# Natural query order, one store per unit, and a reordered seven-product step in a fused attention and MLP kernel

## The chip, the cores and the metric

The kernel runs on one core of one Trainium2 chip. The time is device microseconds of one execution. A profile's *span* is the core's own busy interval in one profiled execution and is one or two microseconds shorter than the run's time (315.5 against 317.19 us for the changed kernel). All readings below compare fast runs with fast runs. A *ratio* is the mean time of one kernel's fast runs over that of the other's fast runs of the same rounds, so it is not quite the ratio of the medians that stand beside it.

## The reference

Sliding-window attention over 8 batches of 576 positions, 8 heads of 64, then a two-layer MLP on the 4608 resulting rows.

```python
def _attn_ref(q, k, v):                       # (8, 8, 576, 64) each
    scores = (1/sqrt(D)) * q @ k^T
    scores = where(|pos_q - pos_k| <= 32, scores, -1e9)
    attn = softmax(scores)
    return attn @ v

def _moe_ref(x, w_in, w_out):                 # x (4608, 512), w_in (512, 2048), w_out (2048, 512)
    h = x @ w_in
    g = h * sigmoid(1.702 * h)
    return g @ w_out
```

## The kernel before

The rows are cut into 36 *units* of 128 and 18 *pairs* of units (a tile of 256 rows). A step of the main loop (`window(w)`, here "pair w") computes attention of pair w, the second layer of pair w−2, and the first layer of pair w−1. Queries are transposed in four groups (`JT = 4`, row = 4s + j), so the scores of a block of 64 queries come out ordered by (j, s) and not by row.

Before, that permuted order was kept through to the output, and the store undid it in two DMAs of 64 rows:

```python
    def scores(self, u):                     # (matmuls cut)
        for eo in range(2):
            if u < self.NU - 1:
                nc.scalar.activation(p[:, eo], sc[eo], AF.Exp, scale=self.scale)
            else: ...                        # last unit: reordered while writing

    def store(self, u, cols=slice(None)):
        nc, row = self.nc, 128 * u + 32
        o_sb = self.o_sb[u]
        if u < self.NU - 1:
            for blk in range(2):
                nc.sync.dma_start(self.out[row + 64*blk:row + 64*blk + 64, cols]
                                      .rearrange("(s j) f -> j s f", j=JT),
                                  o_sb[64*blk:64*blk + 64, cols])
```

The second layer uses seven products instead of eight (a Strassen-like scheme), on sums of `w_out` made once and sums of `g` made per pair on VectorE. Products 1, 6, 7 and 4 accumulate in one PSUM bank and are copied out ("kept") in between, so product 6 must wait until product 1 has been copied, 7 until 6 has, and 4 until 7 has. Products 5 and 3 accumulate in a second bank. Product 2 has a third. The banks have kinds: "a" has four, "h" two, "o" and "t" one each. The first layer takes the two "h" banks in turn.

```python
        self.scores(a); self.scores(b)
        self.product(t, 1, "o"); self.keep(t, 1, dve)
        self.product(t, 5, "h")              # stays in one of the two "h" banks ...
        self.gelu_table()
        self.product(t, 6)
        self.band(a, 0); self.keep(t, 6, dve); self.band(a, 1)
        run(kt)                              # key transposes, bank "t", copied by VectorE
        self.product(t, 2, "h")
        self.band(b, 0); self.result(t, 11); self.band(b, 1)
        self.product(t, 7); self.keep(t, 7, dve)
        self.values(a); self.values(b)
        self.result(t, 22)
        self.product(t, 4); self.result(t, 21, act)
        self.norm(a); self.x_T(a); self.norm(b); self.x_T(b)    # xT: DMA transposes
        self.product(t, 3); self.result(t, 12)                  # ... until here
        run(kt)
        run(l1, 4); self.feed(w); run(l1, 4)                    # first layer, banks "h"
        self.g_sums(w - 1, 1)
```

The softmax here doesn't subtract the row's maximum and nothing guards it: scores larger than these inputs give would overflow.

## Time and profile before

| | before |
|---|---|
| median time | 337.4 us (336.82 to 338.03) |
| TensorE busy | 303.0 us of a 336.6 us span |
| VectorE, ScalarE busy | 212.6, 186.5 us |

These lines of the page of the kernel before carry the rest (group lines: line, engine, operation, tiles, shapes, count, then busy time, mean ns of one, idle time before them and its main releaser; queue lines: packets, MB, time of the packets as a share of 16 engines' span):

```profile
span 336.6 us, 9950 instructions
...
q1 hardware_dynamic: 31296, 16.19, 36.8%
...
L312 PE MATMUL h_ps<-xT,w_in_sb 128*128 128x256 bf16 x1152 | 134.7, 274 | 10.0 <-DMA xT<-x 8.7
...
out_dram<-o_sb SPq DMA_DIRECT2D x68, 128.0 KB
```

TensorE waits 8.7 us ahead of the first layer for transposed activations. The queue that carries stores and transposes (q1) moves 16.19 MB and takes 36.8% of the engines' time for it. The stores are 68 of 128 KB. The pauses of TensorE themselves are shown in the prediction.

### The profile page before, as it was taken

To read this page: it belongs to the slowest core of one execution; us is meant where nothing else is said; L and a number is where in the kernel's file an instruction comes from. 1 tells how busy PE (TensorE), PEld (TensorE's weight loads), DVE (VectorE), ACT (ScalarE), POOL (GpSimd) and SP (SyncE) were. 2 spreads that over 40 slices of the span, in tenths; PEclk is the share of its full clock that TensorE was granted. 3 is DMA by queue.
4 is the path that set the end of the run, shared out by engine and by line. 5 is a ranking of instruction groups with operands and counts; after the bars stand their busy time and mean duration, and the time that the engine had idled before them with its cause. 6 is when DMAs were issued, how large, how long until landed. Compare 5 with 4: busy or idle time off the path is not lost. (4 is left out here: it accounts for less than half of the span.)

```text
span 336.6 us, 9950 instructions
## 1 busy us (share of the span) xinstructions
PE 303.0 (90%) x4224; PEld 247.6 (74%) x4224; DVE 212.6 (63%) x637; ACT 186.5 (55%) x300; POOL 71.2 (21%) x105
## 2 busy tenths in 40 slices
PE   8989999769779969994998899999999999999993
PEld 4668655657668758873887688878888888878882
DVE  2561157788586828683586848686777758583451
ACT  3566354565655638470657365747484847585330
POOL 8972566206014200501040202020200000000000
PEclk9999999999999999998999999999999999999998
DMA  8999999959919996799949994777493442405013
GB/s 141 147 191 203 186 196 189 201 76 122 125 39 134 110 106 91 70 135 102 137 32 146 104 141 47 99 99 97 36 99 84 68 50 48 67 30 72 24 38 89
DMA packets 92684, 35.11 MB, mean 104 GB/s; under 512 B 65248, under 2 KB 88288, under 8 KB 92640
## 3 DMA queue, kind: packets, MB, share of 16 engines
q0 software_dynamic: 61248, 18.22, 57.4%
q1 hardware_dynamic: 31296, 16.19, 36.8%
q8 instruction: 33, 0.54, 0.7%
q14 instruction: 11, 0.09, 0.1%
q10 hardware_dynamic: 96, 0.07, 0.1%
HBM read 36.96 MB, written 9.44 MB: 138 GB/s over the span
## 5 line engine op out<-in xcount | busy, mean ns | idle before, releaser
L312 PE MATMUL h_ps<-xT,w_in_sb 128*128 128x256 bf16 x1152 | 134.7, 274 | 10.0 <-DMA xT<-x 8.7
L312 PEld LDWEIGHTS <-w_in_sb 128*128 128x128 bf16 x1152 | 111.9, 98 | 26.2 <-issue 6.3
L314 ACT ACTIVATE g<-h_ps 128x512 f16<-128x512 f32 x144 | 85.8, 597 | 76.2 <-PE h_ps L312 74.8
L140 POOL DMA_DIRECT2D ve<-in_v_dram x40 | 33.7, 849 | 157.7 <-DVE p L256 114.0
L373 PEld LDWEIGHTS <-gs 128*128 128x128 f16 x512 | 49.7, 98 | 14.3 <-issue 8.6
L373 PE MATMUL o_ps<-w_sum,gs 128*128 128x256 f16 x384 | 49.1, 272 | 6.2 <-DVE part L106 4.8
L353 DVE TENSOR_TENSOR gs<-g 128x512 f16<-128x512 f16 x32 | 13.5, 423 | 63.7 <-ACT g L314 63.6
L241 ACT ACTIVATE p<-sc 128x512 bf16<-128x512 f32 x70 | 36.6, 601 | 6.7 <-PE sc L235 6.4
L106 DVE COPY kT<-tp 128x512 bf16<-128x512 bf16 (+2 forms) x45 | 25.9, 593 | 22.2 <-PE tp L160 20.0
L373 PEld LDWEIGHTS <-g 128*128 128x128 f16 x384 | 34.8, 98 | 4.9 <-ACT g L314 0.2
L373 PE MATMUL o_ps<-w_out_sb,g 128*128 128x256 f16 x256 | 33.3, 273 | 0.0
L284 DVE TENSOR_TENSOR x<-pv,rec 128x256 bf16<-128x256 f32 x72 | 30.6, 425 | 2.5
L106 DVE COPY part<-o_ps 128x256 f32<-128x256 f32 x48 | 20.2, 420 | 15.0 <-PE o_ps L373 14.4
L256 DVE TENSOR_TENSOR p<-p,mask 128x512 bf16<-128x512 bf16 x70 | 28.3, 419 | 1.9 <-ACT p L241 1.6
L106 ACT COPY o_sb<-o_ps 128x256 f32<-128x256 f32 x16 | 6.0, 372 | 37.6 <-PE o_ps L373 30.7
L391 DVE TENSOR_TENSOR o_sb<-o_ps,part 128x256 f32<-128x256 f32 x48 | 20.1, 420 | 0.9 <-PE o_ps L373 0.2
L241 ACT ACT_TABLE_LOAD x15 | 19.2, 1283 | 0.3
L272 PEld LDWEIGHTS <-p 128*64 128x64 bf16 x576 | 12.0, 110 | 9.7 <-DVE p L256 4.2
L272 PE MATMUL pv<-ve,p 128*64 128x65 bf16 x288 | 15.9, 197 | 2.8 <-DVE p L256 1.4
L106 ACT COPY qT<-tp 128x512 bf16<-128x512 bf16 (+1 forms) x17 | 9.6, 573 | 15.4 <-PE tp L160 12.9
L412 ACT ACT_TABLE_LOAD x14 | 18.0, 1283 | 0.3
L235 PEld LDWEIGHTS <-kT 64*64 64x64 bf16 x1152 | 12.1, 108 | 7.6 <-issue 7.2
(68 smaller groups left out, 293.4 us busy)
## 6 DMA issues: line engine op xcount, KB each, us to landing
out_dram<-o_sb SPq DMA_DIRECT2D x68, 128.0 KB
ve<-in_v_dram POOLq DMA_DIRECT2D x32, 128.0 KB, 9.6
w_in_sb<-in_moe_w_in_dram POOLq DMA_DIRECT2D x4, 512.0 KB, 9.7
w_out_sb<-in_moe_w_out_dram POOLq DMA_DIRECT2D x4, 512.0 KB, 12.2
ks<-in_k_dram POOLq DMA_DIRECT2D x2, 448.0 KB, 14.5
qs<-in_q_dram POOLq DMA_DIRECT2D x2, 448.0 KB, 19.4
ks<-in_k_dram POOLq DMA_DIRECT2D x3, 256.0 KB, 17.5
qs<-in_q_dram POOLq DMA_DIRECT2D x3, 256.0 KB, 12.1
```

Source lines behind the costliest of these rows:

```text
L106: (eng.copy if eng is self.nc.scalar else eng.tensor_copy)(out, in_)
L140: self.nc.gpsimd.dma_start(self.ve[m % NV][off:off + n, :, :self.D], self.v[b, :, s:s + n, :].rearrange("h s d -> s h d"))
L241: nc.scalar.activation(p[:, eo], sc[eo], AF.Exp, scale=self.scale)
L256: self.nc.vector.tensor_mul(pv, pv, msk.to_broadcast([128, 4, 2, SQ]))
L272: nc.tensor.matmul(acc[half][blk * 64:blk * 64 + 64, hh, :], p[:, h % 2, h // 2 * 2 + blk, :], vt[:, h, :D + 1], start=(hh == 0), stop=(hh ...
L284: nc.vector.tensor_mul(x[:, hs, :], acc[half][:, :, :D], rec[:, hs, :].to_broadcast([128, 4, D]))
L312: nc.tensor.matmul(hps[:, i, :], self.w_in_sb[:, kr, ff * 128:(ff + 1) * 128], self.xT[t][:, kr, :], start=(i == 0 and kr == 0), stop=(i = ...
L314: nc.scalar.activation(self.g[t][:, ffs[0]:ffs[1] + 1:ffs[1] - ffs[0], :], hps, AF.Gelu_apprx_sigmoid)
L353: dve.tensor_add(s[0], g[:, top, v], g[:, low, v])
L373: nc.tensor.matmul(self.part[t, key], x, y, start=(first and k == 0), stop=(k == 7), skip_group_check=True)
L391: self.nc.vector.tensor_add(dst, self.part[t, src], self.part[t, other])
L412: self.nc.scalar.activation(self.spark, self.spark, AF.Gelu_apprx_sigmoid)
```

## The change

The intent: let ScalarE put the queries back in natural order while it computes the exponential (it reads PSUM at a stride), so that a unit's output is 128 plain rows and one store; put the products in an order that leaves more time to copy each kept product; do both key transposes of a step in one bank and copy them on ScalarE, which is less loaded; make the sums of `w_out` earlier.

```diff
 def scores(self, u):
-            if u < self.NU - 1:
-                nc.scalar.activation(p[:, eo], sc[eo], AF.Exp, scale=self.scale)
-            else: ...
+            nc.scalar.activation(p[:, eo].rearrange("k h (s j) -> k h s j", j=JT),
+                                 sc[eo].rearrange("k h (j s) -> k h s j", j=JT), AF.Exp, scale=self.scale)
 def store(self, u, cols):
-            for blk in range(2):
-                nc.sync.dma_start(self.out[row + 64*blk:row + 64*blk + 64, cols].rearrange("(s j) f -> j s f", j=JT),
-                                  o_sb[64*blk:64*blk + 64, cols])
+            nc.sync.dma_start(self.out[row:row + 128, cols], o_sb[:, cols])
 def head(self):                  # masks in natural order, loads of w_out reordered: cut
+        for n in range(4):       # early, where VectorE idles
+            self.w_sums(n, 0)
 ...
+        for n in range(4):       # after the norm of unit 6
+            self.w_sums(n, 1)
 ...                              # among the key transposes of block 2
-            for half in range(2):
-                self.w_sums(hp, half)
 def window(self, w):             # pairs 5 to 15; pair 4 is changed alike
+        self.g_sums(t, 1, (0, 1))
         self.product(t, 1, "o"); self.keep(t, 1, dve)
-        self.product(t, 5, "h")
+        self.product(t, 2, "h")
+        self.g_sums(t, 1, (2, 3))
+        self.result(t, 11)
         self.gelu_table()
+        self.product(t, 5, "t")
+        self.band(a)
         self.product(t, 6)
-        self.band(a, 0); self.keep(t, 6, dve); self.band(a, 1)
-        run(kt)
-        self.product(t, 2, "h")
-        self.band(b, 0); self.result(t, 11); self.band(b, 1)
+        self.band(b, 0); self.keep(t, 6, dve); self.band(b, 1)
+        self.values(a)
+        if heads:
+            self.keys_pair(heads, act)       # both key transposes, one bank of kind "h"
         self.product(t, 7); self.keep(t, 7, dve)
-        self.values(a)
         self.values(b)
         self.result(t, 22)
         self.product(t, 4); self.result(t, 21, act)
         self.norm(a); self.x_T(a)
+        self.product(t, 3); self.result(t, 12)
         self.norm(b); self.x_T(b)
-        self.product(t, 3); self.result(t, 12)
-        run(kt)
-        run(l1, 4); self.feed(w); run(l1, 4)
-        self.g_sums(w - 1, 1)
+        run(l1, 4); self.g_sums(w - 1, 0); self.feed(w); run(l1, 4)
```

More of the change, by code (lines that the diff above doesn't have):

```diff
@@ L93, in setup_mask @@
         for blks, rows, sign in ((slice(0, 2), lo, 1), (slice(0, 2), hi, -1), (slice(2, 4), lo, -1), (slice(2, 4), hi, 1)):
-            ap = m[rows, blks, :].rearrange("p b (j s) -> p b j s", j=JT)
+            ap = m[rows, blks, :]
             pool.affine_select(out=ap, in_=ap, compare_op=ALU.is_ge, fill=0.0, base=0,
-                               pattern=[[0, 2], [-sign, JT], [-sign * JT, SQ // JT]], channel_multiplier=sign)
+                               pattern=[[0, 2], [-sign, SQ]], channel_multiplier=sign)
     def cut_mask(self):
-        cut = self.mask.rearrange("p b (j s) -> p b j s", j=JT)
         lo, hi = slice(0, 64), slice(64, 128)
-        for b, rows, cols in ((0, hi, slice(0, 8)), (0, lo, slice(8, 16)), (2, lo, slice(0, 8)), (2, hi, slice(8, 16))):
-            self.nc.gpsimd.memset(cut[rows, b, :, cols], 0.0)
+        for b, rows, cols in ((0, hi, slice(0, 32)), (0, lo, slice(32, 64)), (2, lo, slice(0, 32)), (2, hi, slice(32, 64))):
+            self.nc.gpsimd.memset(self.mask[rows, b, cols], 0.0)
     def cast(self, eng, out, in_):
@@ L239, in scores @@
         for eo in range(2):
-            if u < self.NU - 1:
-                nc.scalar.activation(p[:, eo], sc[eo], AF.Exp, scale=self.scale)
-            else:
-                nc.scalar.activation(p[:, eo].rearrange("k h (s j) -> k h j s", j=JT),
-                                     sc[eo].rearrange("k h (j s) -> k h j s", j=JT), AF.Exp, scale=self.scale)
+            nc.scalar.activation(p[:, eo].rearrange("k h (s j) -> k h s j", j=JT),
+                                 sc[eo].rearrange("k h (j s) -> k h s j", j=JT), AF.Exp, scale=self.scale)
         self.p[u] = p
@@ L252, in band @@
         for eo in range(2) if only is None else (only,):
-            if u < self.NU - 1:
-                pv = p[:, eo].rearrange("p (h b) s -> p h b s", b=2)
-                msk = self.mask[:, a:b + 1:b - a, :].rearrange("p (o b) s -> p o b s", o=1)
-                self.nc.vector.tensor_mul(pv, pv, msk.to_broadcast([128, 4, 2, SQ]))
-            else:
-                for blk, m in ((0, a), (1, b)):
-                    pv = p[:, eo, blk::2, :].rearrange("p h (s j) -> p h s j", j=JT)
-                    msk = self.mask[:, m:m + 1, :].rearrange("p o (j s) -> p o s j", j=JT)
-                    self.nc.vector.tensor_mul(pv, pv, msk.to_broadcast([128, 4, SQ // JT, JT]))
+            pv = p[:, eo].rearrange("p (h b) s -> p h b s", b=2)
+            msk = self.mask[:, a:b + 1:b - a, :].rearrange("p (o b) s -> p o b s", o=1)
+            self.nc.vector.tensor_mul(pv, pv, msk.to_broadcast([128, 4, 2, SQ]))
     def values(self, u, kinds="aa"):
@@ L314, in layer1 @@
         nc.scalar.activation(self.g[t][:, ffs[0]:ffs[1] + 1:ffs[1] - ffs[0], :], hps, AF.Gelu_apprx_sigmoid)
-        if t > 1 and d == 3:
+        if t == 2 and d == 3:
             self.g_sums(t, 0)
@@ L323, in layer2 @@
         o_ps = self.o_ps[u]
-        for ff in range(4 * quarter, 4 * quarter + 4):
+        at = (0, 8, 4, 12)[quarter]
+        for ff in range(at, at + 4):
             nc.tensor.matmul(o_ps, self.g[t][:, ff, s * 128:(s + 1) * 128], self.w_out_sb[:, ff, :],
@@ L329, in layer2 @@
             self.cast(eng or nc.vector, o_sb, o_ps)
-            row = 128 * u + 32
-            for blk in range(2):
-                nc.sync.dma_start(self.out[row + 64 * blk:row + 64 * blk + 64, :].rearrange("(s j) f -> j s f", j=JT),
-                                  o_sb[64 * blk:64 * blk + 64])
+            nc.sync.dma_start(self.out[128 * u + 32:128 * u + 160, :], o_sb)
     def w_sums(self, i, half):
@@ L343, in w_sums, with g_sums @@
         dve.tensor_sub(t[i], a, c)
-    def g_sums(self, t, half):
+    def g_sums(self, t, half, which=range(4)):
         dve, g = self.nc.vector, self.g[t]
-        if half == 0:
+        if t not in self.gs:
             self.gs[t] = self.work.tile([128, 4, self.NFF // 2, 128], F16, name="gs", tag="gs")
@@ L352, in g_sums @@
         u, v = slice(0, 128), slice(128, 256)
-        dve.tensor_add(s[0], g[:, top, v], g[:, low, v])
-        dve.tensor_sub(s[1], s[0], g[:, top, u])
-        dve.tensor_sub(s[2], g[:, top, u], g[:, top, v])
-        dve.tensor_sub(s[3], g[:, low, u], s[1])
+        for n in which:
+            if n == 0:
+                dve.tensor_add(s[0], g[:, top, v], g[:, low, v])
+            elif n == 1:
+                dve.tensor_sub(s[1], s[0], g[:, top, u])
+            elif n == 2:
+                dve.tensor_sub(s[2], g[:, top, u], g[:, top, v])
+            else:
+                dve.tensor_sub(s[3], g[:, low, u], s[1])
     def product(self, t, n, kind=None):
@@ L401, in store @@
         if u < self.NU - 1:
-            for blk in range(2):
-                nc.sync.dma_start(self.out[row + 64 * blk:row + 64 * blk + 64, cols].rearrange("(s j) f -> j s f", j=JT),
-                                  o_sb[64 * blk:64 * blk + 64, cols])
+            nc.sync.dma_start(self.out[row:row + 128, cols], o_sb[:, cols])
         else:
@@ L445, in head @@
         self.cut_mask()
-        for c in range(2):
+        for c in (0, 2):
             self.load_w_out(c)
@@ L449, in head @@
             self.load_heads(1, c)
-        self.load_w_out(2)
+        self.load_w_out(1)
         self.load_v(4, 1)
@@ L551, in head @@
             self.queries_T(2, hp, "o", act)
-            for half in range(2):
-                self.w_sums(hp, half)
             self.layer1(2, 4 + hp)
-        self.g_sums(2, 1)
-        for m in (7, 8, 9):
-            self.odd_v(m, dve)
+        self.odd_v(7, dve)
+        self.g_sums(2, 1, (0, 1))
         for m in (11, 12, 13):
@@ L595, in window @@
             self.keep(t, 1, dve)
-            self.product(t, 5, "h")
+            self.product(t, 2, "h")
+            self.g_sums(2, 1, (2, 3))
+            self.result(t, 11)
+            self.product(t, 5, "t")
+            self.band(7)
             self.product(t, 6)
+            self.odd_v(8, dve)
             self.keep(t, 6, dve)
-            self.band(7)
             self.scores(b)
-            self.product(t, 2, "h")
+            self.values(7)
+            self.odd_v(9, dve)
+            self.norm(7)
             self.band(a)
-            self.result(t, 11)
-            self.values(7)
-            self.norm(7)
+            self.product(t, 7)
             self.gelu_table()
+            self.keep(t, 7, dve)
+            self.result(t, 22)
+            self.values(a)
             self.band(b)
-            self.product(t, 7)
-            self.keep(t, 7, dve)
-            self.values(a)
-            self.values(b)
-            self.result(t, 22)
             self.product(t, 4)
             self.result(t, 21, act)
+            self.values(b)
+            self.product(t, 3)
+            self.result(t, 12)
             self.x_T(7, "t", nc.scalar)
@@ L619, in window @@
             self.x_T(b)
-            self.product(t, 3)
-            self.result(t, 12)
             loads()
@@ L631, in window @@
                 run(l1)
-            self.g_sums(w - 1, 1)
+            self.g_sums(w - 1, 0)
             self.feed(w)
@@ L641, in window @@
             self.scores(b)
+        self.g_sums(t, 1, (0, 1))
         self.product(t, 1, "o")
         self.keep(t, 1, dve)
-        self.product(t, 5, "h")
+        self.product(t, 2, "h")
         if w == 5:
             self.scores(b)
+        self.g_sums(t, 1, (2, 3))
+        self.result(t, 11)
         self.gelu_table()
+        self.product(t, 5, "t")
+        self.band(a)
         self.product(t, 6)
-        self.band(a, 0)
+        self.band(b, 0)
         self.keep(t, 6, dve)
-        self.band(a, 1)
-        run(kt)
-        self.product(t, 2, "h")
-        self.band(b, 0)
-        self.result(t, 11)
         self.band(b, 1)
+        self.values(a)
+        if heads:
+            self.keys_pair(heads, act)
         self.product(t, 7)
         self.keep(t, 7, dve)
-        self.values(a)
         self.values(b)
@@ L665, in window, with keys_pair @@
         self.x_T(a)
+        self.product(t, 3)
+        self.result(t, 12)
         self.norm(b)
         self.x_T(b)
-        self.product(t, 3)
-        self.result(t, 12)
-        run(kt)
         run(l1, 4)
+        self.g_sums(w - 1, 0)
         self.feed(w)
         run(l1, 4)
-        self.g_sums(w - 1, 1)
+    def keys_pair(self, heads, eng):
+        i, at = heads[0][0], (512 * heads[0][0]) % RING
+        tp = self.bank("h", [128, 2, JT, 128], BF16, "tp")
+        for n, (_, hp) in enumerate(heads):
+            for j in range(JT):
+                self.nc.tensor.transpose(tp[:, n, j, :], self.stage["k", i, "c"][:, hp, j], self.ident)
+        for n, (_, hp) in enumerate(heads):
+            for dst, m in ((at, 512),) + (((RING, 64),) if at == 0 else ()):
+                self.cast(eng, self.kT[:, hp, dst:dst + m].rearrange("r (p j) -> r p j", j=JT),
+                          tp[:, n, :, :m // JT].rearrange("r j p -> r p j"))
     def close(self, w, l1):
@@ L679, in close @@
         last = not l1
+        self.g_sums(t, 1)
         for n, kind in ((1, "o"), (2, "a"), (6, None), (5, "a"), (7, None)):
@@ L690, in close @@
             l1.pop(0)()
+        if l1:
+            self.g_sums(w - 1, 0)
         if not last:
@@ L694, in close @@
             l1.pop(0)()
-            self.g_sums(w - 1, 1)
             self.product(t, 3)
```

## The prediction

How much faster one store of 128 plain rows drains than two of 64 permuted rows had been seen in no run. That a strided read of PSUM costs ScalarE nothing rested on the 379 ns of its copy of 256 elements at a stride of 8 bytes; in the same trace a dense copy of 256 elements took it 372 ns. The group lines in the middle have the columns named above. L241 is the dense exponential (601 ns), L243 the one that writes at a stride of 8 bytes (1375 ns), and kT<-tp a copy by VectorE that reads at a stride of 256 bytes (685 ns, where its copies of 512 without a stride took 422 ns in bf16 and 682 ns in f32).

> **What bounds the kernel now.** I read the page's engine line, then the kernel in stretches of one pair of query units (I number them as the main loop does, 4 to 19), then TensorE's timeline where it stands still, then the queue of transfers behind those places. Pairs 6 to 11 (columns after the stretch: its length, then busy time of PE, PEld, DVE, ACT, POOL, granted clock, DMA share, GB/s):
>
> ```profile
> PE 303.0 (90%) x4224; PEld 247.6 (74%) x4224; DVE 212.6 (63%) x637; ACT 186.5 (55%) x300; POOL 71.2 (21%) x105
> ```
> ```profile
> 109.20:128.30 19.10, 15.52 (x225) 13.29 (x224) 12.05 (x39) 9.98 (x16) 1.76 (x2) 1.00 1.66 115
> 128.30:144.30 16.00, 15.59 (x230) 13.42 (x229) 11.56 (x36) 9.98 (x16) 4.94 (x7) 1.00 0.60 77
> 144.30:166.30 22.00, 17.06 (x229) 14.13 (x232) 12.11 (x40) 9.98 (x16) 1.77 (x2) 0.92 1.68 124
> 166.30:182.10 15.80, 15.51 (x229) 13.30 (x230) 11.73 (x38) 9.98 (x16) 3.50 (x4) 1.00 0.76 86
> 182.10:200.50 18.40, 15.69 (x225) 13.20 (x224) 12.35 (x41) 10.07 (x16) 1.76 (x2) 1.00 1.61 118
> 200.50:216.40 15.90, 15.53 (x225) 13.37 (x224) 11.73 (x37) 9.98 (x16) 2.25 (x3) 1.00 0.65 78
> ```
>
> TensorE is the bound: 15.5 us of matmuls in every pair, and a normal pair lasts 16. DVE and ACT have room, so only TensorE's pauses count. Every second pair is longer with the same work, at twice the DMA share. Its pauses:
>
> ```profile
> 121.25 4.00 PE L312 MATMUL h_ps<-xT,w_in_sb 128*128 128x256 bf16 x35 [2.97 <-DMA xT<-x]
> ```
> ```profile
> 157.72 8.61 PE L312 MATMUL h_ps<-xT,w_in_sb 128*128 128x256 bf16 x64 [4.35 <-DMA xT<-x]
> ```
> ```profile
> 193.44 0.83 PE L312 MATMUL h_ps<-xT,w_in_sb 128*128 128x256 bf16 x6 [1.41 <-DMA xT<-x]
> ```
>
> All three wait for the transposed activations xT, a DMA transpose. After the longest, 64 first-layer matmuls spread over 8.34 us instead of 6.99, with 3.4 us of half clock in the clock record. Together 2.97 + 4.35 + 1.35 + 1.41 = 10.1 us. Two more pauses come early, where DVE is behind:
>
> ```profile
> 73.53 1.03 PE L373 MATMUL o_ps<-w_sum,gs 128*128 128x256 f16 x8 [2.55 <-DVE part L106]
> ```
> ```profile
> 87.62 0.40 PE L157 MATMUL tp<-ident,kc 128*128 128x128 bf16 x4 [1.69 <-DVE kT L106]
> ```
>
> Later pairs lose 0.1 to 1.2 us each, before product 5 or 6. Why xT is late, from SP's queue ahead of the 4.35 us pause:
>
> ```profile
> 136.58 1.12 SPq L403 DMA_DIRECT2D out_dram<-o_sb  x2
> 137.81 5.86 SPq L295 DMA_TRANSPOSE xT<-x  x2
> 143.77 1.12 SPq L403 DMA_DIRECT2D out_dram<-o_sb  x2
> 145.61 11.22 SPq L198 DMA_TRANSPOSE qT<-qc  x1
> ```
>
> The trace's packets say more. The first two stores' 128 packets of 2 KB run from 138.4 to 146.0 us, the next two's from 151.2 to 156.2, with only 2.6 to 2.7 in flight. The transpose packets do not start before 143.9, and almost stop between 153 and 156, while the stores drain. Of the second xT's 16 completion counts, ten come at 152.1 us and six only at 156.6 to 157.7.
>
> [...] Each store's DRAM side starts with the dimension of 4[...] (after issue one early update of a store's semaphore, then exactly four).
> [...]
> [...]
> [...]
>
> ```profile
> L241 ACT ACTIVATE p<-sc 128x512 bf16<-128x512 f32 x70 | 36.6, 601 | 6.7 <-PE sc L235 6.4
> ...
> L106 DVE COPY kT<-tp 128x512 bf16<-128x512 bf16 x36 | 24.6, 685 | 22.2 <-PE tp L160 20.0 <-PE tp L157 2.2
> ...
> L243 ACT ACTIVATE p<-sc 128x512 bf16<-128x512 f32 x2 | 2.5, 1375 | 0.0
> ...
> L106 ACT COPY qT<-tp 128x256 bf16<-128x256 bf16 x1 | 0.4, 379 | 0.0
> ```
>
> **The change part by part.**
> Stores. Rows come out in natural order, so two stores of 64 permuted rows become one of 128 plain rows[...]. The bytes stay. The 7.6 and 5 us of draining should fall to 1 or 2, transposes start some 3 us sooner, and the stop at 153 goes. Ten counts of xT were there at 152.1, before the need at 153.15; without the stop the other six should be too. I take 85% of 10.1 us (the loads of q and k, which fill these pairs, stay): -8.6.
>
> Exponentials. They now read PSUM at a stride of 64 bytes and write densely. The copy line of 379 ns read at 8 bytes stride at full rate[...], so I take 601 ns: 0. Unit 35's two slow exponentials go (2 x 0.77) and its four half masks become two whole ones, 4 x 0.586 - 2 x 0.419 = 1.5 us of DVE: inside pair 17 below.
>
> Sums of w_out. Eight DVE operations of 0.683 us stood between the key copies at 63 to 69.7 us, so DVE entered pair 4 late; the sums of g, three shifted copies of v and the first kept product came behind (2.55 us). Now four run around 31 to 36 us, where DVE idles 13.5 us (the needed second w_out load lands at 33.5), and four near 57 to 60, where it idles 1.84. Pair 4's sequence by hand with the trace's durations: product 6 no longer waits, but product 7 waits about 0.35 and the values of unit 8 about 1.6 for norm and mask behind two more copies. From scores to first layer 10.5 us instead of 12.5: -2.0. The 1.69 us pause came of the g sums placed inside that first layer; they move behind it: -1.7. Two pauses of 0.19 among the key transposes of block 2 go: -0.4. Sum -4.1.
>
> Pair 5. Its second scores wait for a small wrap copy at the end of DVE's list, before and after (1.68 us before). By hand I get 1.0 there, 0.9 before the values and 0.4 later: +0.5.
>
> Product order in pairs 6 to 14. Product 2 now precedes 5 and 6, so the kept copy of product 1 is no longer waited for. But one unit's values (0.25 us), not two, lie between product 7 and product 4. A kept copy turns around in 0.31 (product end) + 0.42 + about 0.1 = 0.83 us; 0.25 + 0.11 + 0.03 covers 0.39: a new pause of 0.4 a pair. Before, these nine pairs lost 4.6 us (0.55, 0.41, 0.60, 0.29, 1.25, 0.37, 0.60, 0.16, 0.38); after 9 x 0.45 = 4.05: -0.5.
>
> Key transposes. Both blocks go to one bank, together under product 7's wait, and are copied by ACT: 20 copies of 685 ns leave DVE, 20 of about 585 reach ACT, 1.2 us a pair on an engine with 6 us free: 0. In pairs 15 to 17 there are no key transposes to cover product 7's wait either: 0.85 a pair after, against 0.1, 0.1 and 1.0 before: +1.35.
>
> End. In the last pair the second half of the g sums now follows a result instead of preceding it, so the kept product comes about 0.4 us later: +0.4.
>
> Sum: -8.6 - 4.1 + 0.5 - 0.5 + 1.35 + 0.4 = -10.95. From 337.4: 326.4, say 326.3 us.
>
> **Rivals.**
> Strided reads are slow: if ACT needs 1.3 us an exponential, four last 5.2 us instead of 2.1 in each pair, values wait in 14 pairs, 1.5 us or more each, and the time is near 347. For: [...]the 1375 ns. Against: that one is the write side[...].
> The loads hold xT anyway: pairs 6, 8 and 10 hold both loads of q and k, at a DMA share over 1.6. If they, not the stores, bind, xT gains only 2 or 3 us and the time is 332 to 333. Against: ten of sixteen counts came in time, and odd pairs with the same transposes never wait.
> The early part gains nothing: DVE's work in pair 4 is larger by two copies of v; then some 330.
>
> **Range and chances.** Main term uncertain by 3 us, early part by 2, product order by 2, strided reads a separate tail. Range 320.5 to 332.5. Over 2% faster means under 330.65: 0.82; within 2%: 0.12; slower: 0.06.
>
> **What would show it.** Right: store packets 8 or more in flight; no pause "DMA xT<-x" over 0.5 us in pairs 6, 8 and 10, and no half clock there; exponentials at about 600 ns; DVE busy near 196 us, ACT near 197; pair 4 shorter by some 3.7 us; a pause near 0.4 us before product 4. Wrong: exponentials over 800 ns; pauses for xT that remain while stores are spread; a new wait for the values in every pair.

## The result, and the profile after

The changed kernel took 316.12 us (median of four, 315.69 to 317.19) against 337.37 us of the kernel before in the same rounds; the ratio is 0.9374, interval 0.9346 to 0.9403. The direction was right, but the time lies below the predicted range: 21 us were gained where 11 were predicted.

The page of the changed kernel, the lines that answer to those of before:

```profile
span 315.5 us, 9889 instructions
...
PE 297.6 (94%) x4224; PEld 245.8 (78%) x4224; DVE 201.5 (64%) x611; ACT 195.5 (62%) x324; POOL 71.3 (23%) x105
...
q1 hardware_dynamic: 31584, 16.19, 24.7%
...
L302 PE MATMUL h_ps<-xT,w_in_sb 128*128 128x256 bf16 x1152 | 131.9, 273 | 2.3 <-ACT p L239 0.7
...
L239 ACT ACTIVATE p<-sc 128x512 bf16<-128x512 f32 x72 | 37.5, 602 | 3.8 <-PE sc L234 3.6
...
out_dram<-o_sb SPq DMA_DIRECT2D x34, 256.0 KB, 3.5
```

The first layer no longer waits for xT (10.0 us of idle time before it became 2.3). The same 16.19 MB on queue q1 now take 24.7% of the engines' time instead of 36.8%. A store of 256 KB lands 3.5 us after it is issued. The exponentials read PSUM at a stride of 64 bytes and take 602 ns, where the dense ones took 601 and the two that wrote at a stride of 8 bytes 1375. ScalarE's new key copies read PSUM at a stride of 256 bytes and take 582 ns, where its copies of the same size without a stride take 584 to 585.

Pairs 6 to 11 in stretches (columns: stretch, length, busy PE, PEld, DVE, ACT, POOL, granted clock, DMA share, GB/s):

```profile
105.60:121.90 16.30, 15.47 (x225) 13.33 (x224) 11.03 (x38) 11.06 (x18) 1.76 (x2) 1.00 1.31 170
121.90:137.40 15.50, 15.36 (x229) 13.33 (x228) 10.48 (x34) 10.94 (x18) 4.94 (x7) 1.00 0.81 75
137.40:152.90 15.50, 15.36 (x229) 13.33 (x230) 11.08 (x38) 10.94 (x18) 1.77 (x2) 1.00 1.43 166
152.90:168.30 15.40, 15.26 (x225) 13.27 (x224) 10.39 (x33) 11.17 (x20) 3.50 (x4) 1.00 0.76 80
168.30:183.80 15.50, 15.36 (x226) 13.32 (x224) 11.04 (x37) 11.17 (x20) 1.75 (x2) 1.00 1.16 161
183.80:199.60 15.80, 15.48 (x225) 13.36 (x224) 10.59 (x34) 11.05 (x18) 2.24 (x3) 1.00 0.46 68
```

The even pairs, which lasted 19.1, 22.0 and 18.4 us, now last 16.3, 15.5 and 15.5, at a higher byte rate, and the half clock of pair 8 is gone. The odd pairs are 0.1 to 0.5 us shorter too. The trace's packets of 2 KB on queue q1, which are the stores', tell the same: between 100 and 300 us, while any was under way, 3.2 were under way together before and 8.8 after. A store's semaphore, too, is updated more often as it lands: 16 times for each of the 40 stores after, and five times, one of them early, for each of the 68 of 64 rows before.

The Sync engine's queue of the changed kernel in pairs 7 and 8, to be held against the same queue in the prediction:

```profile
130.03 0.33 SPq L395 DMA_DIRECT2D out_dram<-o_sb  x1
130.47 1.26 SPq L285 DMA_TRANSPOSE xT<-x  x1
131.82 1.44 SPq L395 DMA_DIRECT2D out_dram<-o_sb  x1
133.36 2.09 SPq L285 DMA_TRANSPOSE xT<-x  x1
138.72 5.58 SPq L197 DMA_TRANSPOSE qT<-qc  x1
```

The transposes are no longer held on the queue behind stores: the two of xT occupied it for 5.86 us before and for 1.26 + 2.09 us now, that of qT for 11.22 and now for 5.58. The loads of q and k probably still slow them, though no run tests that by itself: while those loads run, the two of xT land 10.0 and 12.0 us after their issue (130.47 to 140.44, 133.36 to 145.39), where from pair 10 on the recorded landings take 2.4 to 4.3. In the changed kernel the second is just early enough for its use at 145.79.

Lengths in us, measured from the start of one pair's scores to the next pair's, read from the two traces and from that of the experiment `e1_natural_order_alone`, which comes below:

| pair | 4 | 5 | 6 | 7 | 8 | 9 | 10 | 11 | 12 to 14 (sum) | 15 | 16 | 17* | last TensorE work to end |
|---|---|---|---|---|---|---|---|---|---|---|---|---|---|
| before | 23.31 | 17.49 | 19.17 | 15.93 | 21.99 | 15.81 | 18.46 | 15.88 | 47.89 | 15.16 | 15.17 | 17.33 | 5.98 |
| natural order alone | 23.32 | 17.49 | 16.14 | 15.68 | 16.12 | 15.81 | 16.26 | 15.76 | 47.90 | 15.16 | 15.16 | 16.04 | 3.81 |
| changed | 20.58 | 17.09 | 16.33 | 15.48 | 15.48 | 15.48 | 15.48 | 15.81 | 46.44 | 15.23 | 15.22 | 16.20 | 3.82 |

(*pair 17: to the start of the first layer of its own rows. The last column counts from the start of TensorE's last matmul.) The rest is before pair 4 (68.37 us before, 67.91 after) and from the start of pair 17's first layer to the start of the last matmul (18.71 and 18.96).

### The profile page after: what moved, and what is told of

Same layout as the page of the kernel before. It is cut to its first block, busy times and chain, and to the rows that moved or that the text cites.

```text
span 315.5 us, 9889 instructions
## 1 busy us (share of the span) xinstructions
PE 297.6 (94%) x4224; PEld 245.8 (78%) x4224; DVE 201.5 (64%) x611; ACT 195.5 (62%) x324; POOL 71.3 (23%) x105
## 3 DMA queue, kind: packets, MB, share of 16 engines
q1 hardware_dynamic: 31584, 16.19, 24.7%
## 5 line engine op out<-in xcount | busy, mean ns | idle before, releaser
L302 PE MATMUL h_ps<-xT,w_in_sb 128*128 128x256 bf16 x1152 | 131.9, 273 | 2.3 <-ACT p L239 0.7
L366 PE MATMUL o_ps<-w_sum,gs 128*128 128x256 f16 x384 | 47.2, 273 | 1.0 <-DVE part L105 0.6
L366 PEld LDWEIGHTS <-g 128*128 128x128 f16 x384 | 36.2, 97 | 6.7 <-ACT g L304 0.2
L239 ACT ACTIVATE p<-sc 128x512 bf16<-128x512 f32 x72 | 37.5, 602 | 3.8 <-PE sc L234 3.6
L366 PE MATMUL o_ps<-w_out_sb,g 128*128 128x256 f16 x256 | 31.0, 273 | 0.0
L384 DVE TENSOR_TENSOR o_sb<-o_ps,part 128x256 f32<-128x256 f32 x48 | 20.3, 423 | 11.1 <-PE o_ps L366 10.3
L105 ACT COPY o_sb<-o_ps 128x256 f32<-128x256 f32 x16 | 6.0, 372 | 26.3 <-PE o_ps L366 19.1
L105 DVE COPY kT<-tp 128x512 bf16<-128x512 bf16 (+2 forms) x21 | 11.8, 580 | 15.6 <-PE tp L159 12.2
L366 PE MATMUL o_ps<-w_sum,g 128*128 128x256 f16 x128 | 16.6, 272 | 1.8
L105 ACT COPY qT<-tp 128x512 bf16<-128x512 bf16 (+1 forms) x17 | 9.6, 572 | 12.2 <-PE tp L159 11.7
## 6 DMA issues: line engine op xcount, KB each, us to landing
ks<-in_k_dram POOLq DMA_DIRECT2D x2, 448.0 KB, 11.2
```

What stands on the lines that cost most here:

```text
L105: (eng.copy if eng is self.nc.scalar else eng.tensor_copy)(out, in_)
L239: nc.scalar.activation(p[:, eo].rearrange("k h (s j) -> k h s j", j=JT), sc[eo].rearrange("k h (j s) -> k h s j", j=JT), AF.Exp, scale=sel ...
L302: nc.tensor.matmul(hps[:, i, :], self.w_in_sb[:, kr, ff * 128:(ff + 1) * 128], self.xT[t][:, kr, :], start=(i == 0 and kr == 0), stop=(i = ...
L366: nc.tensor.matmul(self.part[t, key], x, y, start=(first and k == 0), stop=(k == 7), skip_group_check=True)
L384: self.nc.vector.tensor_add(dst, self.part[t, src], self.part[t, other])
```

## The experiments

Theory A, the prediction's: the stores on four DMA engines hold up the transposes, and everything else is small. Rival B: the loads of q and k hold xT, and the reordering did the work. Rival C: the stores cost more than the xT waits show. Rival D: the products gain by something that the prediction did not count. Twelve kernels ran in three batches; each batch has its own runs of the kernel before (medians 339.21, 339.61 and 338.3 us), so ratios are the safer comparison across batches.

### 1. Natural order alone

The kernel before, with only the natural query order, its masks and the single store:

```diff
-                nc.scalar.activation(p[:, eo], sc[eo], AF.Exp, scale=self.scale)
+            nc.scalar.activation(p[:, eo].rearrange("k h (s j) -> k h s j", j=JT),
+                                 sc[eo].rearrange("k h (j s) -> k h s j", j=JT), AF.Exp, scale=self.scale)
-            for blk in range(2): ...two stores of 64 permuted rows
+            nc.sync.dma_start(self.out[row:row + 128, cols], o_sb[:, cols])
```

> The kernel before with the natural query order alone (exponentials written dense, plain masks, one store of 128 rows a unit); window order, key copies and sums of w_out as before. Theory (stores on 4 of 16 engines hold up the transposes): the three pauses for xT (2.97, 4.35, 1.41 us) and the 1.35 us of half clock go, -10.1; the last stores land some 1.6 us sooner; the pair with the slow exponentials of the last unit is 1.1 us shorter: about 324.5 us. Rival (the loads of q and k hold xT): the pauses mostly stay, 332 us or more.

Measured 323.56 us (322.33 to 323.82), ratio 0.9527 (0.9461 to 0.9592), span 320.6: as expected by theory A. The first layer's line of its page:

```profile
L302 PE MATMUL h_ps<-xT,w_in_sb 128*128 128x256 bf16 x1152 | 133.6, 273 | 1.1 <-ACT g L304 0.7
```

No wait for xT is left. This part alone is worth 336.6 − 320.6 = 16.0 us of span. The table above says where: pairs 6, 8 and 10 lose 3.03 + 5.87 + 2.20 = 11.1 us, pair 17 1.3 us (the slow exponentials and half masks of the last unit), the end behind TensorE's last work 2.2 us, and the stretch before pair 4 1.1 us. That last item is not to be trusted: two runs of the same changed kernel differ by 0.9 us there (67.91 and 67.05).

### 2. Permuted order and two stores put back into the changed kernel

```diff
-                nc.sync.dma_start(self.out[row:row + 128, cols], o_sb[:, cols])
+                for blk in range(2):
+                    nc.sync.dma_start(self.out[row+64*blk:row+64*blk+64, cols].rearrange("(s j) f -> j s f", j=JT),
+                                      o_sb[64*blk:64*blk+64, cols])
```
(with the old masks and exponentials)

> The changed kernel with the permuted query order put back (permuted masks, two stores of 64 rows a unit, strided exponentials for the last unit); everything else changed. Theory: pauses for xT come back in pairs 6, 8 and 10 and the tail is 1.6 us longer: 327 to 330 us. Rival (the new step itself keeps TensorE off the transposes, stores don't matter): within 2 us of the changed kernel, 316 to 318.

Measured 344.22 us, but the runs scatter from 337.45 to 350.14. Three of the four count as slow, the profiled one too; only that of 337.45 counts as fast, so no ratio is given. 327 to 330 were expected. The direction agrees with A and C. That the changed kernel with the old stores should be no faster than the kernel before was unexpected, and called for a cleaner test.

### 3 to 5. One store of 256 KB on 4, 8 and 16 engines

The changed kernel with nothing but the view of the store's DRAM side changed. The rows come out in the wrong places; the bytes, the stores' 4352 packets of 2 KB, the loads and all other instructions stay.

```diff
-            nc.sync.dma_start(self.out[row:row + 128, cols], o_sb[:, cols])
+            nc.sync.dma_start(self.out[row:row + 128, cols].rearrange("(s j) f -> j s f", j=4), o_sb[:, cols])
```
(and j=8, j=16)

> The changed kernel with its one store of 128 rows a unit, but the rows of the output addressed as 4 groups of 32, so that the slowest dimension is 4; the rows land permuted (a wrong result on purpose), bytes and instruction count unchanged. Theory (number of engines): pauses as with two permuted stores, 326 to 330 us. Rival (the number of stores, or SP's issue time, matters): 316 to 317.

> The same wrong-row store, but addressed as 16 groups of 8 rows: the rows are scattered just as badly, the slowest dimension is 16. Theory (number of engines): as the changed kernel, 316 us within 1. Rival (the scattered rows in DRAM matter, not the engines): as with 4 groups, 326 to 330.

> The changed kernel with the wrong-row store addressed as 8 groups of 16 rows (8 engines). Theory (the load on the busiest engine counts): between 317.7 (16 engines) and 344 (4 engines), nearer to 16: 318 to 323 us.

| outer dimension | median us | lowest to highest | ratio to before | span |
|---|---|---|---|---|
| 4 | 344.05 | 342.25 to 346.30 | 1.0141 (1.0060 to 1.0222) | 344.6 |
| 8 | 321.00 | 320.88 to 324.43 | 0.9518 (0.9450 to 0.9586) | 319.3 |
| 16 | 317.71 | 316.61 to 320.22 | 0.9372 (0.9297 to 0.9447) | 318.5 |

The outer dimension alone moves the time by 26 us, far more than the 10 to 14 us expected for 4 groups (326 to 330 us). That refutes rival B as the cause of the waits: loads, bytes and order of products are the same in all three. It also says that what the outer dimension changes in a store carries the largest part, and that 8 groups are already most of the way. The traces show what it changes. 36 stores were changed, and queue q1 has 432 = 36 × 12 packets of 4 bytes fewer with 4 groups than with 16, and 288 = 36 × 8 fewer with 8; and 3.3, 5.5 and 8.4 packets of 2 KB are under way together with 4, 8 and 16. The traces name no engine for a packet. "Stores on 4, 8 and 16 engines" is the reading of these counts, one 4-byte packet for a store and engine, and of the updates of the semaphore (four after the early one before, 16 after). From the page of the kernel with 4:

```profile
span 344.6 us, 9889 instructions
...
q1 hardware_dynamic: 31152, 16.19, 36.5%
```

The queue's share is back at 36.5% with the bytes unchanged. TensorE's timeline of that run, the pauses alone (start, length, engine, line, tiles, count, and in brackets the idle time before and what ended it):

```profile
95.74 1.56 PE L366 MATMUL o_ps<-w_sum,gs 128*128 128x256 f16 x10 [3.32 <-issue]
...
191.93 0.19 PE L262 MATMUL pv<-vo,p 128*64 128x65 bf16 x1 [3.33 <-issue]
```
and its waits (total, times, longest):

```profile
PE h_ps L302 <- DMA xT<-x: 7.6, 2, 4.7
PE sc L234 <- DMA qT<-qc: 3.6, 1, 3.6
PE pv L262 <- issue: 3.3, 1, 3.3
PE o_ps L366 <- issue: 3.3, 1, 3.3
PE tp L678 <- issue: 2.3, 1, 2.3
```

Waits for transposes come to 7.6 + 3.6 = 11.2 us; that is what late transposes cost directly. Three more pauses, 3.3 + 3.3 + 2.3 = 8.9 us, have no semaphore behind them ("issue"): one falls in the middle of a product whose operands were all there. And the clock record has four stretches of half clock, 3.4 us each, one after each of the pauses of 3.32, 3.33, 3.58 and 4.7 us; TensorE's busy time is 304.3 us against 298.7 with 16 engines. With an end 1.4 us longer, and less the 1.8 us that the 16-engine run pauses in the second way, these parts make up the 26 us but for 1.

Counted in TensorE's instructions, the three places without a semaphore are 511 and 1792 apart. The page lists an instruction queue of 33 packets, 0.54 MB, which is 16 KB a packet; such a packet ended 1.3 us before TensorE went on in the first of these pauses, and 2.5 and 4.1 us before in the others. No run here changed those packets, so what TensorE waits for in these pauses is not shown. That stores on few engines cause them is not shown either, for at the very same instruction of pair 6 TensorE paused with 16 and with 8 engines too:

```profile
112.11 0.55 PE L678 MATMUL tp<-ident,kc 128*128 128x128 bf16 x7 [1.78 <-issue]
```
```profile
112.23 0.55 PE L678 MATMUL tp<-ident,kc 128*128 128x128 bf16 x7 [2.60 <-issue]
```

In the changed kernel the pause there is 0.69 us, and another run of the same kernel had none over 0.2 there and a pair 6 shorter by 0.56 us. Only at the two other places are such pauses seen with 4 engines alone.

### 6. Sums of w_out in the old place

```diff
-        for n in range(4): self.w_sums(n, 0)      # early
-        for n in range(4): self.w_sums(n, 1)
+            for half in range(2): self.w_sums(hp, half)   # among the key transposes of block 2
```
(with the old order of w_out's loads)

> The changed kernel with the eight sums of w_out back among the key transposes of block 2, and w_out loaded and used in the old order. Theory (the early sums are what lets DVE enter pair 4 on time): pair 4 and the stretch before it 2 to 3 us longer, all later pairs unchanged: 318 to 319.5 us. Rival (the new order of products and copies in pair 4 absorbs DVE's lateness): within 0.7 us of the changed kernel.

Measured 318.36 us (317.37 to 320.63), ratio 0.9411, span 318.9. Pair 4 took 24.52 us instead of 20.58, and apart from scatter in pairs 6 and 10 the other pairs stayed. But the profiled execution is the slowest of the four, and it alone had a granted clock below 1.0 (0.989): 6.8 us of half clock lie in its pair 4, where TensorE is busy for 21.18 us instead of 18.46. So 2.7 of the 3.9 us are the clock, and 1.2 are waits. The three runs at full clock (317.37 to 318.42) lie 1.3 to 2.3 us above the changed kernel's median; that is about what the place of the sums is worth.

### 7. Old order of products, new banks

```diff
-            self.product(t, 2, "h"); ...; self.product(t, 5, "t"); self.product(t, 6)
+            self.product(t, 5, "t"); self.product(t, 6); ...; self.keys_pair(heads, act); self.product(t, 2, "h")
-            self.values(a)                 # before product 7
+            self.values(a)                 # behind product 7, with unit b's
-            product 3 and its result between the two norms
+            product 3 and its result behind both
```
(pairs 5 to 17 only; cut: all four sums of g go ahead of product 1 again, and the masks to their old places)

> The changed kernel with the old order of the seven products, masks and values from pair 5 on (product 5 before 6 and 2, both units' values together, all four g sums ahead), key copies by ScalarE and stores as changed. Theory after the trace (a pause of only 0.14 us before product 4 against 0.1 to 0.55 before product 6): pairs 6 to 14 longer by 0.2 to 0.6 us each, pairs 15 to 17 shorter by 0.1: 318 to 320 us. The prediction's sizes (0.4 us a pause, 0.85 in pairs 15 to 17) would make it 314 to 315.

Measured 315.79 us (315.58 to 319.67), ratio 0.9362 (0.9274 to 0.9451), span 314.0 against 315.5. The expectation of a longer run was wrong. Pair by pair the old order is shorter by 0.36 to 0.46 us in pairs 15, 16 and 17, longer by 0.46 in pair 5, and alternates around the new one (15.31 and 15.75 against 15.48) in most others: pairs 5 to 17 together are 1.2 us shorter. 0.56 of that is pair 6, which differs by as much between two runs of the changed kernel (experiment 12). So what is firm is that the new order of products, taken by itself, costs 0.37 + 0.36 + 0.46 = 1.19 us in pairs 15 to 17, and gains nothing in pairs 6 to 14 together (140.49 us in the changed kernel, 139.93 in its second run, 140.05 here).

### 8. Product 5 in an "h" bank again

The kernel of experiment 7 with two letters exchanged:

```diff
-        self.product(t, 5, "t")
+        self.product(t, 5, "h")
-        tp = self.bank("h", [128, 2, JT, 128], BF16, "tp")     # keys_pair
+        tp = self.bank("t", [128, 2, JT, 128], BF16, "tp")
```

> The kernel with the old product order (key copies by ScalarE, stores as changed), with two PSUM banks exchanged: product 5 back in one of the two banks that the first layer uses, the key transposes in the single one. Theory (product 5's accumulator held a first-layer bank until the pair's last result, and the second group of the first layer waited for it): about 0.1 us more in pairs 5 to 14, 0.3 in pairs 15 to 17, some 2 us more than the 315.8 of the old order run. Rival (the bank does not matter, only the key copies' engine): within 0.7 us of it.

Measured 319.61 us (319.33 to 319.8), ratio 0.9443 (0.9396 to 0.9491), span 317.7 against 314.0 of experiment 7. The intervals of the two ratios just overlap (0.9396 and 0.9451), so the proof is in the pairs: each of pairs 5 to 17 is longer by 0.29 to 0.31 us, 3.9 us in all, where 2 were expected. Pairs 15 to 17, which have no key transposes, are longer by the same 0.3, so it is product 5's bank and not that of the keys. The first layer's line of experiment 7 and then of this one:

```profile
L302 PE MATMUL h_ps<-xT,w_in_sb 128*128 128x256 bf16 x1152 | 131.9, 273 | 1.4 <-ACT xT L105 0.7 <-ACT g L304 0.7
```
```profile
L302 PE MATMUL h_ps<-xT,w_in_sb 128*128 128x256 bf16 x1152 | 134.0, 273 | 4.1 <-ACT p L239 0.7 <-ACT xT L105 0.7 <-ACT g L304 0.7
```

Where it sits is seen in the timeline of this kernel at the start of pair 15's first layer:

```profile
257.05 0.41 DVE L384 TENSOR_TENSOR o_sb<-o_ps,part 128x256 f32<-128x256 f32 x1
...
257.52 1.08 PEld L302 LDWEIGHTS <-w_in_sb 128*128 128x128 bf16 x10 [0.31 <-issue]
```

The addition that ends the seven-product step reads product 5's bank until 257.46 us; the weight loads of the first layer's second group of eight matmuls begin at 257.52. The first group used the other "h" bank; the second needs the one that product 5 and 3 have just left. In the trace its first matmul starts 0.41 us after the last of the first group; in experiment 7, with product 5 in "t", it starts after the usual 0.11. In the kernel before the same step is 0.21 to 0.23 us in most of pairs 5 to 14, where a group of key transposes stood between and hid part of it, and 0.41 to 0.46 in pairs 15 to 17. The label "issue" names no bank, so this wait is visible only as a step in the start times.

### 9. Key copies by VectorE

```diff
-            self.keys_pair(heads, act)
+            self.keys_pair(heads, dve)
```

> The changed kernel with the two key copies of each pair 5 to 14 on VectorE instead of ScalarE, still in one bank. Theory (they get into the way of the kept copy of product 7, which product 4 waits for): 0.3 to 0.5 us a pair, 319 to 321 us. Rival (VectorE has room): within 0.7 us of the changed kernel.

Measured 320.58 us (320.1 to 322.75), ratio 0.9479 (0.9416 to 0.9543), span 318.4. Most of pairs 5 to 14 last 15.80 instead of 15.48 us, +0.32. The prediction put the key copies at 0. By this run they are worth 0.3 us a pair in the new order. The likely reason, argued from the program's order and not tested by itself, is that VectorE's two copies (0.69 us each) then stand ahead of the copy of product 7.

### 10. Filling the pauses with first-layer work

One group of the first layer was drawn forward ahead of product 4 in pairs from 6 on, and another ahead of product 7 in pairs 15 to 17:

```diff
+        if fill and not heads: run(l1)
         self.product(t, 7)
 ...
+        if fill: run(l1)
         self.product(t, 4)
```
(cut; the first layer behind has that many groups fewer)

> The changed kernel with one group of the first layer moved between the second unit's values and product 4, and in pairs 15 to 17 another before product 7. Theory (product 4 waits 0.14 us for a kept copy that nothing covers, 12 pairs, and product 7 as much in three): 1.5 to 2 us less, minus up to 1.5 in pair 8 where the transposes land only 0.4 us before their use: 314.5 to 316. If the pause is TensorE's own cost of switching and no wait, no change.

Measured 315.55 us (315.06 to 316.24), ratio 0.9320 (0.9263 to 0.9377), span 314.3. A normal pair takes 15.28 instead of 15.48 us, but xT is now needed sooner, and two pairs wait for it; from the waits of this run:

```profile
PE h_ps L302 <- DMA xT<-x: 2.5, 2, 1.4
```

The transposes are thus only just off the path in the changed kernel: the second xT of pair 8 lands 0.4 us before its use (145.39 against 145.79 in the trace).

### 11. A third order of products, combined

The order 1, 2, 6, 5, keys, 7, values of both units, 4, 3: product 5 lies between product 6 and the wait of product 7, and all values between product 7 and the wait of product 4. The sums of `g` ahead of pair 4 are spread among the key transposes.

```diff
-        if t == 2 and d == 3: self.g_sums(t, 0)
+            self.g_sums(2, 0, (hp,))       # one for each head pair of block 2
-        self.product(t, 5, "t"); self.band(a); self.product(t, 6); ...
+        self.product(t, 6); self.band(a, 0); self.keep(t, 6, dve); self.product(t, 5, "t"); self.band(a, 1)
-        self.values(a)                     # before keys_pair
+        self.values(a)                     # behind keep(t, 7), with unit b's
```

(cut; unit b's masks come behind the key transposes, and both norms ahead of product 3)

> The changed kernel with the products of pairs 5 to 17 in a third order (1, 2, 6, 5, keys, 7, both units' values, 4, 3), so that another product or the values lie between each kept copy and its use, and with the first half of the g sums of tile 2 spread between the key transposes of block 2. Theory (each pause is a kept copy's turnaround of some 0.8 us that nothing covers): pairs 5 to 14 at 15.2 to 15.3 us, the 1.33 us pause before pair 4 gone: 310 to 312.5 us. If the kept copy only comes later because VectorE is behind, as the old order: 314 to 316.

Measured **308.95 us** (308.2 to 309.49, six runs), ratio 0.9125 (0.9087 to 0.9163), span 306.5, correct. It beats both kernels, and the expected range too. Two things were changed at once; the lengths tell them apart: the stretch before pair 4 is 65.53 us against 67.91 and 67.05, and pairs 5 to 17 together are 6.0 us shorter than in the changed kernel's second run. Two of its pairs:

```profile
103.00:118.10 15.10, 15.10 (x229) 13.25 (x228) 10.93 (x38) 10.94 (x18) 1.76 (x2) 1.00 1.43 170
118.10:133.10 15.00, 15.00 (x225) 13.24 (x224) 10.30 (x33) 10.94 (x18) 4.94 (x7) 1.00 0.68 75
```

TensorE is busy for the whole stretch; what is left of a pair is TensorE's own work. Nearly all pairs from 6 to 14 last 15.06 to 15.09 us, so the changed kernel's 15.48 holds 0.4 us of loss a pair.

### 12. The changed kernel again

No edit; it ran on the same chip as experiments 8 and 11 and the store on 8 engines.

> The changed kernel itself, as a yardstick on this chip: 316 to 317 us.

Measured 316.19 us (315.13 to 317.57, six runs), ratio 0.9346 (0.9305 to 0.9387), span 314.1. The gain is reproduced, and the span of the one program moved by 1.4 us: 0.9 of it before pair 4, 0.56 in pair 6.

## Why the prediction was wrong

The direction and the main mechanism were right. The size was half of the truth. The terms against what the traces give (us; "stores" from before to natural order alone, "products and keys" from there to the changed kernel):

| term | predicted | measured |
|---|---|---|
| stores, pairs 6 to 14 | −8.6 | −11.4 |
| stores, behind TensorE's last work | not in the sum | −2.2 |
| pair 4 | −3.7 | −2.7 |
| pair 5 | +0.5 | −0.4 |
| products and keys, pairs 6 to 14 | −0.5 | −3.2 |
| pairs 15 to 17 | +1.35 | −1.0 |
| behind pair 17's first layer | +0.4 | +0.25 |
| before pair 4 | −0.4 | −0.5 (within scatter) |
| sum | −10.95 | −21.1 |

**Stores, the first failed term.** The step "I take 85% of 10.1 us (the loads of q and k, which fill these pairs, stay): -8.6" was too small in two ways. Nothing of the waits stayed, and pairs 6, 8 and 10 gave up 11.1 us, one more than their listed pauses, the rest small losses in other pairs. And the sum looked only at xT, not at the last stores, which the kernel must wait for. In the trace before they landed at 335.65 us, now at 314.26, and the end behind TensorE's last work shrank from 5.98 to 3.82 us. The mechanism held: with the natural order alone no wait for xT is left, and experiments 3 to 5 change only the outer dimension of a store (4, 8, 16), and 11.2 us of waits for transposes come and go with them.

**Products and keys, the second failed term.** "4.6 … after 9 x 0.45 = 4.05: -0.5" and "Key transposes. … : 0" came to −3.2 together, for two reasons. First, the list of pauses of the kernel before covered the products and not the start of the first layer, where product 5's bank cost 0.11 us in most of pairs 5 to 14 and 0.3 in each of 15 to 17. The change moves product 5 to a bank that the first layer does not use. The step for the key transposes read that exchange of banks as one of engines only. With the banks put back but everything else of the keys' move left in place, pairs 5 to 17 together are only 0.55 us shorter than with the natural order alone (experiment 8 against experiment 1). The banks add 3.9 there (8 against 7), and the new order of products takes back 1.2 (7 against the changed kernel, 0.56 of it scatter in pair 6): 0.55 + 3.9 − 1.2 = 3.3 us, the measured gain of those pairs over experiment 1 (3.2 in pairs 6 to 14, 0.4 in pair 5, less 0.3 in 15 to 17). In pairs 6 to 14 alone the same steps are −0.9, −2.7 and +0.4: there the reordering, for which the prediction counted −0.5, gained nothing, and the exchange of banks, for which it counted nothing, gained most. That the three add up is arithmetic, since each kernel is compared with the next; what is shown is each single step. Keys and banks are one term, not two: the old place of the key transposes hid part of the bank wait, which experiment 8 lays bare.

Second, the pause expected before product 4, "a new pause of 0.4 a pair", came out at 0.14 us. From the changed kernel's timeline in pair 8, the last matmul of unit b's values and product 4:

```profile
143.71 0.19 PE L262 MATMUL pv<-vo,p 128*64 128x65 bf16 x1
144.04 1.03 PE L366 MATMUL o_ps<-w_sum,g 128*128 128x256 f16 x8
```

The values end at 143.71 + 0.19 = 143.90, product 4 starts at 144.04. By the prediction's own 0.83 us for a kept copy, and product 4's usual gap, the values and the gaps around them cover about 0.65 us of it (an estimate), not the estimated 0.39. Experiment 11 bounds what is left: with both units' values there, and product 5 ahead of product 7, a pair is 0.4 us shorter still.

**Pairs 15 to 17.** The +1.35 is a net of 3 × 0.75 = +2.25 for the products (0.85 a pair against 0.1) and −0.9 for pair 17's slow exponentials and half masks. The products cost 1.19 (experiment 7), about half of that; pair 17 gained 1.3 by its exponentials and masks (experiment 1); and the bank, which the estimate did not have, took off another 3 × 0.3. That 1.19 lies near the net figure of 1.35 is chance.

**Pair 4.** The first layer there was estimated well: −1.7 predicted, 10.8 to 8.9 us measured. (The −0.4 of the prediction's sum for this part lies before pair 4, at 65.02 and 66.83 us.) From scores to first layer 12.5 us became 11.7, where 10.5 were said. The two pauses that the hand schedule missed are in the changed kernel's timeline:

```profile
78.57 0.38 PE L289 MATMUL tp<-ident,x 128*128 128x128 bf16 x4 [0.52 <-DVE o_sb L384]
79.62 2.56 PE L302 MATMUL h_ps<-xT,w_in_sb 128*128 128x256 bf16 x22 [0.67 <-ACT xT L105]
```

The transposes of unit 7 use bank "t", which product 5 and 3 now hold to the step's end (0.52 us), and since they come behind product 3 nothing covers their copy to SBUF (0.67 us). 0.52 + 0.67 is as much as the missing 1.2. The account is not closed, though: the 1.6 us that the schedule gave to the values' wait came out at 0.81. The 0.52 is the same exchange of banks that paid in the later pairs. **Pair 5** was scheduled by hand as well: its waits are 0.67 and 0.20 us instead of 1.0, 0.9 and 0.4.

**What held.** Exponentials at 602 ns; ScalarE busy 195.5 us against the 197 said; no half clock and no wait for xT in pairs 6, 8 and 10; stores with 8.8 packets under way. VectorE's 201.5 us against 196 did not agree; it bounds nothing, and was not followed up. The prediction's rivals "strided reads are slow" and "the loads hold xT anyway" both fell as causes of lost time (that the transposes land later while the loads run is said above); of those set up for the experiments, B fell with experiments 1 and 3 to 5, and C and D are what theory A lacked.

**Half clock and the pauses.** In the kernel before, the only half clock of the main loop goes with the 4.35 us pause (3.41 us of it, from 157.34 us). By the other runs the length of a pause alone does not decide it: half clock set in after pauses of at most 1.48 us (experiment 6, at 77.9 us) and 1.78 us (16 engines, at 113.1), and none after one of 2.60 us (8 engines).

**What stays open.** What TensorE waits for in the pauses without a semaphore under four-engine stores; why the changed kernel with four-engine stores is slower than the kernel before, which has them too (it has 8.9 us of pauses without a semaphore and four stretches of half clock in the main loop and behind it, the kernel before none and one); what the move of the keys gains beside the bank; and the third of a microsecond by which pair 11 exceeds its neighbours.

## What to carry to other kernels

Before blaming traffic for a late transfer, look at the outer dimension of every store on the same queue: 4, 8 or 16 there made 344, 321 or 318 us with the same bytes. When a change moves operations about, write down for each PSUM bank who holds it and until when, before and after; a wait for a bank can show as a 0.3 us step without a name, once per iteration, and exchanging two letters gained or lost 3.9 us. Where a partial result must be copied out before its bank is used again, put an independent product or all the values, not a fraction of them, between the two: here that took most pairs from 15.48 to between 15.06 and 15.09 us.
